# One attention and expert kernel: weight decoding in 512-column units in the first seven periods, and expert blocks that begin with 128 and 256 tokens

## The chip, the cores and the metric

The kernel runs on one core of one Trainium2 chip. The metric is the device time of one execution in microseconds (us); less is better. The core's engines are named as the profile names them: PE (TensorE, matmuls) and PEld (its weight loads), DVE (VectorE), ACT (ScalarE), POOL (GpSimd) and SP (SyncE, which here issues all transfers).

## The reference

The kernel computes an attention in which each query keeps its 32 largest scores, and feeds the result to a product of four weight matrices. With 8 batches, 8 heads, 576 positions and heads of 64:

```
scores = scale * np.matmul(q, k.transpose(0, 1, 3, 2))
kth = np.partition(scores, -top_k, axis=-1)[..., -top_k:-top_k + 1]
scores = np.where(scores >= kth, scores, -1000000000.0)
attn = softmax(scores)                      # over the keys
x = np.matmul(attn, v), laid out as 4608 tokens x 512
out = ((x @ w1) * (x @ w2)) @ w3 @ w_out    # w1, w2: 512x1024, w3: 1024x1024, w_out: 1024x512
```

The four weights arrive as 64-bit floats, so that the kernel must turn each into a 32-bit one.

## The kernel before

**Periods.** The attention is cut into 144 slots, 18 for each batch: one slot is the work of one pair of heads on 128 queries (of two pairs on the last 64). One loop, `for p in range(-1, n_slots + 3)`, runs one period for each p and is software-pipelined: period p computes the scores of slot p+1 (`scores`, tile `st` on PE, copied to `s` by ACT), finds the 32 largest of slot p (`top32_steps`, tiles `w` and `top` on DVE), masks and exponentiates slot p-1 (`mask` and `exps`, tile `pab`, on ACT and POOL) and turns and multiplies slot p-2 by the values (`turn`, `values`, tiles `tp`, `pts`, `pr`, `ro`), whose result `normalise` scales on DVE. Every engine takes its instructions in program order (class `InOrder`): an instruction that waits holds up all that stand behind it on its engine. In the trace a period begins with the first `w<-s` row of DVE.

**Expert products.** When a block of tokens is complete, `moe_steps` yields its 288 matmuls one by one: 24 groups of 8 times 24 over w1 and w2 (tile `ab`; weights `wh` and `wl`, the high and low parts) and 4 times 24 for the output (tile `eo`, weights `wf`). Before the change all blocks have 12 slots, which is 384 tokens (`NB`, the columns of each matmul). `fill(n)` puts n of these matmuls into the program at three places of a period (`SHARE = 8, 8, 8`), so a block takes 12 periods. Evictions (`take_a`, `take_b`, `take_o`) are put off to the next `fill`. Block 0 is complete at the end of period 13 and begins in period 14; the last block's matmuls run after the last period.

**Decoding.** `startup` lists the weights as units of 256 columns: 16 of w_out, 32 of w3, 16 of w1, 16 of w2. `warm()` is called six times in a period, from period 0 on. Each call starts one unit and moves every unit under way one step further: ACT writes `t` and `r` from the fetched tile `z`; DVE makes sign and magnitude (TENSOR_SCALAR, SCALAR_TENSOR_TENSOR); POOL adds the low part; then PE multiplies a w3 unit by w_out into the PSUM tile `pf` (`load_w3`), or ACT and POOL split a w1 or w2 unit into `wh` and `wl` (`load_w12`). When all of one `pf` is there, ACT copies it to `wf[0]` and DVE subtracts into `wf[1]`. Each of these stages has a `yield` of its own, and there is one more `yield` between POOL's add and the use. The tile `z` comes out of the pool `g`, which the expert products use later, `t` and `pf` out of the PSUM pool `ps_m` of three banks, which they use too.

Of the kernel before, what the change touches and what calls it, by code (L numbers as in the profile page):

```python
# [26 lines left out]
NB = 384  # L27
# [10 lines left out]
BLOCK = NS * NB // S  # L38
# [4 lines left out]
WAITING = 4  # L43
SHARE = 8, 8, 8
# [23 lines left out]
def attn_moe(ctx: ExitStack, tc: tile.TileContext, q, k, v, w1, w2, w3, w_out, out, flag, general):  # L68
# [8 lines left out]
    g_p = ctx.enter_context(tc.tile_pool(name="g", bufs=NFC))  # L77
# [3 lines left out]
    ps_m = ctx.enter_context(tc.tile_pool(name="ps_m", bufs=3, space=PSUM))  # L81
# [18 lines left out]
    def fetch(src):  # L100
        z = g_p.tile([128, 2 * NB], F32, tag="g", name="z")
        sp.dma_start(z[:, :512].bitcast(I32), src)
        return z

    bank = []

    def decode(z, dst=None):
        if not bank:
            both = ps_m.tile([128, 512], F32, tag="mm", name="t")
            bank.extend((both[:, 256:], both[:, :256]))  # L110
        t = bank.pop()
        high = z[:, 1:512:2]
        low = z[:, :512].bitcast(U16)[:, 1:1024:4]
        sign, u, r = (z[:, i * 256 : (i + 1) * 256].bitcast(I32) for i in range(3))
        act.activation(t, high, AF.Copy, scale=2.0**-112)
        act.activation(r, low, AF.Copy, scale=2.0**-13)
        yield
        ti = t.bitcast(I32)
        dve.tensor_scalar(sign, ti, -(2**31), None, op0=ALU.bitwise_and)
        dve.scalar_tensor_tensor(u, ti, 3, sign, op0=ALU.logical_shift_left, op1=ALU.bitwise_or)  # L120
        yield
        dst = z[:, :256] if dst is None else dst
        pool.tensor_tensor(dst.bitcast(I32), u, r, op=ALU.add)
        yield
        yield
        return dst

    def load_w12(i, c, z):
        if len(wl) == i:
            wl.append(const.tile([128, NCC * DF], F32R, tag="wl1", name="wl1"))  # L130
        cut = slice(c * 256, (c + 1) * 256)
        y = yield from decode(z)
        act.copy(wh[i][:, cut], y)
        yield
        pool.tensor_tensor(wl[i][:, cut], y, wh[i][:, cut].bitcast(F32), op=ALU.subtract)
# [6 lines left out]
    def load_w3(c, z):  # L142
        f, i = c // 4, c % 4
        y = yield from decode(z)
        if i == 0:
            fold[f] = ps_m.tile([128, 512], F32, tag="mm", name=f"pf{f}")
        for j in range(2 * i, 2 * i + 2):
            pe.matmul(
                fold[f], y[:, (j % 2) * 128 : (j % 2 + 1) * 128], wo[:, j * DM : (j + 1) * DM],
                start=(j == 0), stop=(j == NFC - 1),  # L150
            )
        if i == 3:
            cut = slice(f * DM, (f + 1) * DM)
            yield
            act.copy(wf[0][:, cut], fold[f])
            yield
            dve.tensor_tensor(wf[1][:, cut], fold[f], wf[0][:, cut].bitcast(F32), op=ALU.subtract)

    startup = [(w_out[c], lambda z, c=c: load_wout(c, z)) for c in range(16)]
    for f in range(NFC):  # L160
        startup += [(w3[c], lambda z, c=c: load_w3(c, z)) for c in range(4 * f, 4 * f + 4)]
        startup += [(w1[c], lambda z, c=c: load_w12(0, c, z)) for c in range(2 * f, 2 * f + 2)]
    startup += [(w2[c], lambda z, c=c: load_w12(1, c, z)) for c in range(16)]
# [171 lines left out]
    def moe_steps(xs, nb, places, after):  # L335
# [34 lines left out]
        for e in range(NEC):  # L370
            p = ps_m.tile([128, 512], F32, tag="mm", name="eo")
# [57 lines left out]
    n_blocks = n_slots // BLOCK  # L429
    column, places = {}, []  # L430
    for n in range(n_blocks):
        mine = sorted({group_of[i] for i in range(n * BLOCK, (n + 1) * BLOCK)}, key=lambda g: groups[g])
# [9 lines left out]
        assert lo == NB  # L442
# [54 lines left out]
    for hp in range(NHP):  # L497
        kts[0, hp] = load_k(0, hp)
        if hp == 0:
            prefetch(WAITING)  # L500
    for hp in range(NHP):
        vts[0, hp] = load_v(0, hp)
    renew_q(1)
    for p in range(-1, n_slots + 3):
        i, j, m = p + 1, p - 1, p - 2
        finder = top32_steps(ss[p], p) if 0 <= p < n_slots else iter(())
# [16 lines left out]
        fill(SHARE[0])  # L523
# [8 lines left out]
        fill(SHARE[1])  # L532
# [20 lines left out]
        fill(SHARE[2])  # L553
        for _ in finder:
            pass
        if 0 <= m < n_slots:
            n = m // BLOCK
# [8 lines left out]
            if (m + 1) % BLOCK == 0:  # L566
# [3 lines left out]
    while queue:  # L570
        fill(6)
# [5 lines left out]
    wp = ps_m.tile([128, 512], F32, tag="mm", name="wp")  # L577
# [57 lines left out]
```

## Time and profile before

| | |
|---|---|
| median of 3 runs (lowest to highest) | 1322.38 us (1319.78 to 1322.73) |
| the profiled execution's own time | 1321.85 us |
| its span, first to last instruction | 1320.0 us |
| PE, DVE, ACT, POOL busy | 94%, 90%, 73%, 65% of the span |
| instructions | 28196 |

The busy share says in which part of the span an engine had an instruction under way. It is a mean over stages: the periods in which weights are decoded, those with expert products beside the attention, and the expert products alone at the end. In the trace period 0 begins at 7.38 us, period 14 at 206.35, period 26 at 304.40.

### The profile page before, as it was taken

What the parts mean: (1) busy time and instruction counts of PE and PEld (TensorE: products, weight loads), DVE (VectorE), ACT (ScalarE), POOL (GpSimd) and SP (SyncE); (2) the same over time, 40 slices, a digit from 0 to 9 for tenths busy, and PEclk for the clock granted to TensorE, in tenths of its full rate; (3) what the DMA queues carried; (4) which work ended last, traced back from release to release, by engine and by line L of the source; (5) the groups of instructions that cost most, each with busy time, mean ns of one, the idle gap of its engine ahead of it and who ended that gap; (6) DMA issues with size and microseconds to landing.
All of it is one profiled execution on the core that took longest, in us unless ns stands there. A gap on an engine that the chain in (4) does not pass through costs nothing.

```text
span 1320.0 us, 28196 instructions
## 1 busy us (share of the span) xinstructions
PE 1235.3 (94%) x9617; PEld 1047.7 (79%) x9617; DVE 1194.1 (90%) x4012; ACT 965.9 (73%) x2057; POOL 853.7 (65%) x1225
## 2 busy tenths in 40 slices
PE   2788858999999999999999999999999999999996
PEld 1334436888888888888888888888888888888996
DVE  7988898999999999999999999999999999999610
ACT  5766786877777877777877877778777778777621
POOL 4767697666766766667757757757667666667510
PEclk9899967999999999999999999999999999999998
DMA  6333331200121001100120012110220012000000
GB/s 243 91 101 123 110 96 29 81 22 21 29 74 32 9 27 64 53 27 16 39 84 20 10 33 79 32 33 10 65 60 9 15 47 81 22 21 1 13 13 27
DMA packets 35886, 64.82 MB, mean 49 GB/s; under 512 B 6036, under 2 KB 12180, under 8 KB 35732
## 3 DMA queue, kind: packets, MB, share of 16 engines
q1 hardware_dynamic: 35732, 62.93, 15.3%
q8 instruction: 77, 1.26, 0.4%
q14 instruction: 77, 0.63, 0.2%
HBM read 53.48 MB, written 9.44 MB: 48 GB/s over the span
## 4 chain that ended last, share of the span: by engine, by line
PE 87%; DVE 4%; POOL 3%; ACT 2%; issue 2%; DMA 1%; SPq 0%; POOLq 0%
PE ab L57 32%; PE eo L57 16%; PE ro L57 15%; PE st L57 12%; PE tp L57 9%; PE pf L57 3%; DVE z L57 2%; DVE w L57 1%; POOL z L57 1%; DVE top L57 1%; POOL wl L57 1%; ACT pab L57 1%; DMA vt<-in_v 0%; ACT s L57 0%; ACT z L57 0%
## 5 line engine op out<-in xcount | busy, mean ns | idle before, releaser
L57 POOL TENSOR_TENSOR pab<-s,pab 128x576 f32<-128x576 f32 x288 | 404.2, 1426 | 127.5 <-DVE w L57 102.0
L57 DVE MAX8 top<-w 128x8 f32<-128x192 f32 (+1 forms) x1152 | 467.3, 447 | 0.0
L57 PE MATMUL ab<-x,wh 128*128 128x384 f32 x1536 | 403.7, 344 | 0.0
L57 ACT COPY pts<-tp 128x1024 f32<-128x1024 f32 x144 | 146.1, 1014 | 198.2 <-PE tp L57 196.8
L57 DVE MATCH_REPLACE8 w<-top,w 128x192 f32<-128x192 f32 x864 | 289.4, 343 | 0.0
L57 PEld LDWEIGHTS ab<-x,wh 128*128 128x128 f32 x1536 | 275.3, 189 | 0.0
L57 PE MATMUL ab<-x,wl 128*128 128x384 f32 x768 | 269.5, 351 | 0.0
L57 ACT ACTIVATE pab<-pab,edge 128x576 f32<-128x576 f32 x288 | 226.8, 787 | 0.5 <-POOL pab L57 0.5
L57 PE MATMUL eo<-g,wf 128*128 128x384 f32 x1152 | 225.8, 346 | 0.0
L57 ACT ACTIVATE pab<-s,edge 128x576 f32<-128x576 f32 x288 | 207.6, 768 | 7.6 <-POOL edge L57 7.5
L57 PE MATMUL st<-kt,qt 64*128 64x288 f32 (+1 forms) x1280 | 188.7, 443 | 18.4 <-ACT pts L57 7.4
L57 PEld LDWEIGHTS eo<-g,wf 128*128 128x128 f32 x1152 | 198.6, 188 | 7.5 <-issue 7.5
L57 ACT COPY s<-st 128x576 f32<-128x576 f32 x288 | 184.4, 640 | 19.5 <-PE st L57 19.5
L57 DVE TENSOR_TENSOR w<-w,s 128x384 f32<-128x384 f32 x288 | 183.9, 639 | 4.9
L57 DVE TENSOR_TENSOR w<-s 128x384 f32<-128x384 f32 x288 | 173.0, 642 | 7.4 <-ACT s L57 7.4
L57 PEld LDWEIGHTS ro<-pts,vt 128*64 128x64 f32 x2560 | 130.2, 139 | 51.3 <-ACT g L57 28.3
L57 PEld LDWEIGHTS st<-kt,qt 64*128 64x128 f32 (+1 forms) x1280 | 100.6, 183 | 81.0 <-ACT pr L57 28.1
L57 PE MATMUL ro<-pts,vt 128*64 128x128 f32 (+1 forms) x2560 | 163.4, 271 | 0.0
L57 PE MATMUL tp<-ident,pab 128*128 128x128 f32 x1152 | 152.1, 275 | 11.3 <-ACT s L57 11.3
L57 PEld LDWEIGHTS ab<-x,wl 128*128 128x128 f32 x768 | 144.3, 188 | 13.4 <-issue 12.3
L57 PEld LDWEIGHTS tp<-ident,pab 128*128 128x128 f32 x1152 | 136.4, 142 | 22.3 <-POOL wo L57 10.7
L57 POOL TENSOR_TENSOR g<-asb,g 128x384 fp32r<-128x384 f32 x96 | 96.9, 1010 | 86.8 <-ACT g L57 86.8
(51 smaller groups left out, 1309.6 us busy)
## 6 DMA issues: line engine op xcount, KB each, us to landing
z<-in_w SPq DMA_DIRECT2D x64, 256.0 KB, 2.7
vt<-in_v SPq DMA_DIRECT2D x32, 352.0 KB, 3.7
qt<-in_q SPq DMA_DIRECT2D x40, 256.0 KB, 2.7
kt<-in_k SPq DMA_DIRECT2D x32, 320.0 KB, 3.1
out_t<-osb SPq DMA_DIRECT2D x32, 192.0 KB, 1.9
z<-in_wo SPq DMA_DIRECT2D x16, 256.0 KB, 3.9
out_t<-osb SPq DMA_DIRECT2D x16, 160.0 KB, 1.8
out_t<-osb SPq DMA_DIRECT2D x16, 32.0 KB, 1.6
```

What stands on the lines that cost most here:

```text
L57: ins = fn(*args, **kw)
```

## The change

Decoding units have 512 columns instead of 256 (`CHUNK`), so there are 40 instead of 80: 8 of w_out, then eight times two of w3 and one of w1, then 8 of w2. They live in pools of their own, `z` (three buffers each of `z`, `r`, `y`) and `ps_e` (two banks of `t`, one of `pf`), which `settle()` closes before the first expert product; `g` and `ps_m` open then. `warm()` also runs in period -1. Several stages of a unit now share one call of `warm()`: DVE's two instructions and POOL's add stand in one step, `wh` and `wl` in another, and the spare `yield` is gone. Keys and values of the first batch are fetched one by one in the first periods instead of all ahead of the loop.

The expert blocks end at the slots in `CUTS`: 0, 4, 12, 24, and so on, so block 0 has 128 tokens, block 1 has 256, the others 384 as before. Each has 288 matmuls still, and `begin` divides them over the fills that lie between its start and the next block's: 12 for each fill for block 0 (periods 6 to 13), 8 for all others.

```
-BLOCK = NS * NB // S
+CUTS = [0, 4] + list(range(NS * NB // S, B * NS + 1, NS * NB // S))
-WAITING = 4
-SHARE = 8, 8, 8
+CHUNK = 512
+WAITING = 3
...
+    early = ExitStack()
+    z_p = early.enter_context(tc.tile_pool(name="z", bufs=WAITING))
+    ps_e = early.enter_context(tc.tile_pool(name="ps_e", bufs=2, space=PSUM))
...
     def decode(z, dst=None):
+        t = ps_e.tile([128, CHUNK], F32, tag="t", name="t")
+        r = z_p.tile([128, CHUNK], I32, tag="r", name="r")
+        act.activation(t, z[:, 1 : 2 * CHUNK : 2], AF.Copy, scale=2.0**-112)
+        act.activation(r, z.bitcast(U16)[:, 1 : 4 * CHUNK : 4], AF.Copy, scale=2.0**-13)
         yield
+        y = z_p.tile([128, CHUNK], F32, tag="y", name="y")
+        ti, yi = t.bitcast(I32), y.bitcast(I32)
+        dve.tensor_scalar(yi, ti, -(2**31), None, op0=ALU.bitwise_and)
+        dve.scalar_tensor_tensor(yi, ti, 3, yi, op0=ALU.logical_shift_left, op1=ALU.bitwise_or)
-        yield
-        dst = z[:, :256] if dst is None else dst
-        pool.tensor_tensor(dst.bitcast(I32), u, r, op=ALU.add)
-        yield
+        dst = y[:] if dst is None else dst
+        pool.tensor_tensor(dst.bitcast(I32), yi, r, op=ALU.add)
         yield
         return dst
...
     def load_w3(c, z):
-        f, i = c // 4, c % 4
+        f, i = c // 2, c % 2
         y = yield from decode(z)
         if i == 0:
-            fold[f] = ps_m.tile([128, 512], F32, tag="mm", name=f"pf{f}")
+            fold[f] = ps_e.tile([128, 512], F32, tag="pf", name=f"pf{f}", bufs=1)
-        if i == 3:
+        if i == 1:
             cut = slice(f * DM, (f + 1) * DM)
             yield
             act.copy(wf[0][:, cut], fold[f])
-            yield
             dve.tensor_tensor(wf[1][:, cut], fold[f], wf[0][:, cut].bitcast(F32), op=ALU.subtract)
...
     def begin():
         while starting:
+            if not late:
+                while going:
+                    warm()
+                settle()
             n = starting.pop(0)
-            queue.append(moe_steps([xs[n, hp] for hp in range(NHP)], NB, places[n], put_off.append))
+            fills = 3 * (CUTS[n + 2] - CUTS[n + 1]) if n + 1 < n_blocks else 36
+            steps = moe_steps([xs[n, hp] for hp in range(NHP)], widths[n], places[n], put_off.append)
+            queue.append((steps, -(-3 * (2 * NCC * NFC + NFC * NEC) // fills)))
...
     def warm():
-        if p < 0:
-            return
```

Where it stands on PE in a period that folds w3 (`pf`, numbered by fold). Before, the rows of one such period:

```order
L57 MATMUL tp_583<-ident_85,pab_434 128x128 x8
L57 MATMUL ro_592<-ident_85,pab_434 128x128
L57 MATMUL ro_592<-ident_85,wide_561 128x128
L57 MATMUL pf1_601<-wo_102,z_426 128x512 x2
L57 MATMUL pf1_601<-wo_102,z_445 128x512 x2
L57 MATMUL st_625<-kt_116,qt_130 128x288 x2
L57 MATMUL st_628<-kt_116,qt_130 128x288 x2
L57 MATMUL ro_592<-pts_595,vt_126 64x128 x8
L57 MATMUL ro_592<-pr_597,vt_126 64x128 x2
L57 MATMUL pf1_601<-wo_102,z_477 128x512 x2
L57 MATMUL pf1_601<-wo_102,z_490 128x512 x2
```

And in the changed kernel, from one fold's first unit to the end of the next fold:

```order
L57 MATMUL pf5_610<-wo_102,y_588 128x512 x4
L57 MATMUL tp_629<-ident_85,pab_441 128x128 x8
L57 MATMUL ro_638<-ident_85,pab_441 128x128
L57 MATMUL ro_638<-ident_85,wide_602 128x128
L57 MATMUL pf5_610<-wo_102,y_615 128x512 x4
L57 MATMUL st_678<-kt_106,qt_185 128x288 x2
L57 MATMUL st_681<-kt_106,qt_185 128x288 x2
L57 MATMUL ro_638<-pts_641,vt_286 64x128 x8
L57 MATMUL ro_638<-pr_643,vt_286 64x128 x2
L57 MATMUL pf6_702<-wo_102,y_668 128x512 x4
L57 MATMUL pf6_702<-wo_102,y_707 128x512 x4
```

A period held eight `pf` matmuls of one fold; it now holds sixteen of two, one fold around `tp` and ahead of `st`, the next behind `ro`.

The same stretch on DVE. Before, the first half of a period:

```order
L57 RECIPROCAL sums<-sums 128x2
L57 TENSOR_TENSOR w<-s 128x2x192 x2
L57 TENSOR_TENSOR w<-w,s 128x2x192 x2
L57 TENSOR_SCALAR z<-t 128x256
L57 SCALAR_TENSOR_TENSOR z<-t,z 128x256
L57 TENSOR_TENSOR wf_101<-pf_601,wf_100 128x512
L57 TENSOR_SCALAR z<-t 128x256
L57 SCALAR_TENSOR_TENSOR z<-t,z 128x256
L57 MAX top_97<-w 128x8 x2
```

In the changed kernel, the second half of a period (`pf_610` is fold 5), up to the next period's RECIPROCAL:

```order
L57 TENSOR_TENSOR wf_101<-pf_610,wf_100 128x512
L57 TENSOR_SCALAR y<-t 128x512
L57 SCALAR_TENSOR_TENSOR y<-t,y 128x512
L57 MAX top_95<-w 128x8 x2
L57 MATCH_REPLACE w<-top_95,w 128x192 x2
L57 TENSOR_SCALAR y<-t 128x512
L57 SCALAR_TENSOR_TENSOR y<-t,y 128x512
L57 MAX top_95<-w 128x8 x2
L57 TENSOR_TENSOR pr<-ro,pr 128x128
L57 TENSOR_SCALAR y<-t 128x512
L57 SCALAR_TENSOR_TENSOR y<-t,y 128x512
L57 RECIPROCAL sums<-sums 128x2
```

The subtraction into `wf`, which needs a whole fold from PE, stood once in a period, right after the first unit; it now stands twice, at the period's beginning and in its middle.

## Rows read from the trace of the kernel before
**Rows 1.** The page of the profiled execution: its span, the busy time of the engines, and from the 40 equal slices the busy tenths of PE and the granted TensorE clock in tenths (PEclk).

```profile
span 1320.0 us, 28196 instructions
...
PE 1235.3 (94%) x9617; PEld 1047.7 (79%) x9617; DVE 1194.1 (90%) x4012; ACT 965.9 (73%) x2057; POOL 853.7 (65%) x1225
...
PE   2788858999999999999999999999999999999996
...
PEclk9899967999999999999999999999999999999998
```

**Rows 2.** Busy time by stage. Columns: the stretch, its length, busy us and instructions of PE, PEld, DVE, ACT and POOL, granted clock, share of the DMA engines, GB/s. The stretches: period 0; periods 4 to 10; periods 11 to 13; period 14; periods 15 to 25; period 26; period 29.

```profile
7.38:18.19 10.81, 4.58 (x16) 2.45 (x16) 10.60 (x35) 4.49 (x12) 2.91 (x4) 1.00 1.04 390
56.78:165.14 108.36, 85.65 (x380) 42.20 (x379) 92.91 (x275) 75.62 (x182) 74.80 (x105) 0.94 0.36 107
165.14:206.35 41.21, 24.02 (x128) 15.22 (x126) 37.38 (x112) 33.01 (x82) 38.47 (x55) 0.63 0.28 77
206.35:216.45 10.10, 7.13 (x40) 5.49 (x41) 7.87 (x27) 5.51 (x10) 6.27 (x10) 0.66 0.08 19
216.45:304.40 87.95, 87.95 (x824) 77.49 (x824) 85.23 (x297) 69.21 (x148) 59.29 (x85) 1.00 0.16 50
304.40:312.33 7.93, 7.93 (x64) 6.99 (x64) 7.55 (x29) 5.91 (x12) 4.40 (x8) 1.00 0.11 33
328.20:336.13 7.93, 7.93 (x64) 7.00 (x63) 7.90 (x30) 6.30 (x13) 6.12 (x10) 1.00 0.01 3
```

**Rows 3.** Groups of instructions in periods 4 to 10 (56.78 to 165.14 us): busy time, mean ns of one, idle time before them and what ended it.

```profile
L57 PE MATMUL pf<-wo,z 128*128 128x512 f32 x114 | 59.8, 660 | 20.5 <-POOL z L57 18.6 <-DVE z L57 1.9
...
L57 POOL TENSOR_TENSOR z<-z 128x256 int32<-128x256 int32 x42 | 31.7, 769 | 17.1 <-ACT x L57 9.7 <-ACT t L57 2.2 <-DVE sums L57 1.7
...
L57 DVE SCALAR_TENSOR_TENSOR z<-t,z 128x256 int32<-128x256 int32 x43 | 18.3, 424 | 1.5
...
L57 DVE TENSOR_SCALAR z<-t 128x256 int32<-128x256 int32 x42 | 17.5, 417 | 5.7 <-ACT z L57 5.7
...
L57 DVE TENSOR_TENSOR wf<-pf,wf 128x512 fp32r<-128x512 f32 x7 | 4.8, 681 | 0.0
...
L57 ACT CAST wf<-pf 128x512 fp32r<-128x512 f32 x7 | 4.1, 587 | 7.2 <-PE pf L57 7.2
```

**Rows 4.** Waits in the same periods: who waited for whom, us in total, how often, the longest.

```profile
PE pf L57 <- POOL z L57: 18.6, 7, 2.9
...
DVE pr L57 <- POOL sums L57: 8.1, 7, 1.9
```

**Rows 5.** The engines in order of time in period 9 (134.40 to 150.59 us). Columns: start, time from the first to the last of a run of equal instructions, engine, operation, out<-in, how many, and in brackets the idle time before and what ended it. A matmul on 32-bit operands stands as two records.

```profile
133.91 2.31 PE L57 MATMUL pf<-wo,z 128*128 128x512 f32 x5
...
135.49 0.51 POOL L57 TENSOR_TENSOR edge<-top,coef 128x4 f32<-128x4 f32 x1
...
136.25 0.59 ACT L57 CAST wf<-pf 128x512 fp32r<-128x512 f32 x1 [1.04 <-PE pf L57]
...
136.83 0.62 POOL L57 COPY wide<-sums 128x128 f32<-128x128 f32 x1
...
138.54 2.77 POOL L57 TENSOR_TENSOR pab<-s,pab 128x576 f32<-128x576 f32 x2 [1.10 <-ACT pab L57]
...
139.39 0.61 DVE L57 MAX8 top<-w 128x8 f32<-128x192 f32 x2
...
140.57 0.41 DVE L57 TENSOR_SCALAR z<-t 128x256 int32<-128x256 int32 x1
...
142.74 3.23 PE L57 MATMUL pf<-wo,z 128*128 128x512 f32 x4 [2.61 <-POOL z L57]
...
145.64 1.41 DVE L57 MAX8 top<-w 128x8 f32<-128x576 f32 x2
...
145.89 1.64 PE L57 MATMUL st<-kt,qt 64*128 64x288 f32 x8
...
150.59 0.54 DVE L57 TENSOR_TENSOR w<-s 128x384 f32<-128x384 f32 x1
```

**Rows 6.** PE and its weight loads in order of time late in the span, with the columns of rows 5: expert products of 384 columns, then the transposes of a slot, then expert products again.

```profile
1202.69 0.52 PE L57 MATMUL ab<-x,wh 128*128 128x384 f32 x2
...
1205.17 0.34 PE L57 MATMUL ab<-x,wl 128*128 128x384 f32 x1
1205.34 1.03 PE L57 MATMUL tp<-ident,pab 128*128 128x128 f32 x8
...
1206.33 0.30 PEld L57 LDWEIGHTS ab<-x,wh 128*128 128x128 f32 x2
```

**Rows 7.** The first microseconds in order of time, with the columns of rows 5 (SPq is the queue of transfers), and the rate of the transfers in 40 slices of the first 30 us.

```profile
1.68 1.84 SPq L57 DMA_DIRECT2D z<-in_wo  x4
...
4.38 2.29 PE L57 MATMUL st<-kt,qt 64*128 64x288 f32 x8 [4.38 <-DMA kt<-in_k]
...
7.24 0.41 ACT L57 ACTIVATE t<-z 128x256 f32<-128x256 f32 x1
...
GB/s 0 0 98 330 383 369 350 399 367 382 386 385 402 398 402 406 399 394 402 393 385 385 385 352 243 172 0 131 219 0 0 0 11 22 167 314 401 194 232 68
```

**Rows 8.** Groups of the whole span, with the columns of rows 3.

```profile
L57 POOL TENSOR_TENSOR pab<-s,pab 128x576 f32<-128x576 f32 x288 | 404.2, 1426 | 127.5 <-DVE w L57 102.0
...
L57 POOL TENSOR_TENSOR g<-asb,g 128x384 fp32r<-128x384 f32 x96 | 96.9, 1010 | 86.8 <-ACT g L57 86.8
```

More of the change, by code (lines that the diff above doesn't have):

```diff
@@ L80, in attn_moe, with settle @@
     ps_v = ctx.enter_context(tc.tile_pool(name="ps_v", bufs=1, space=PSUM))
-    ps_m = ctx.enter_context(tc.tile_pool(name="ps_m", bufs=3, space=PSUM))
+    early = ExitStack()
+    z_p = early.enter_context(tc.tile_pool(name="z", bufs=WAITING))
+    ps_e = early.enter_context(tc.tile_pool(name="ps_e", bufs=2, space=PSUM))
+    late = {}
+    def settle():
+        early.close()
+        late["g"] = ctx.enter_context(tc.tile_pool(name="g", bufs=NFC))
+        late["mm"] = ctx.enter_context(tc.tile_pool(name="ps_m", bufs=3, space=PSUM))
     ident = const.tile([128, 128], F32, name="ident")
@@ L370, in moe_steps @@
         for e in range(NEC):
-            p = ps_m.tile([128, 512], F32, tag="mm", name="eo")
+            p = late["mm"].tile([128, 512], F32, tag="mm", name="eo")
             for f in range(NFC):
@@ L428, in attn_moe @@
         group_of.append(len(groups) - 1)
-    n_blocks = n_slots // BLOCK
-    column, places = {}, []
+    n_blocks = len(CUTS) - 1
+    block_of = [n for n in range(n_blocks) for _ in range(CUTS[n], CUTS[n + 1])]
+    column, places, widths = {}, [], []
     for n in range(n_blocks):
-        mine = sorted({group_of[i] for i in range(n * BLOCK, (n + 1) * BLOCK)}, key=lambda g: groups[g])
+        mine = sorted({group_of[i] for i in range(CUTS[n], CUTS[n + 1])}, key=lambda g: groups[g])
         lo, pieces = 0, []
@@ L451, in evict, with fill @@
             put_off.pop(0)()
-    def fill(n):
+    def fill():
         evict()
+        n = queue[0][1] if queue else 0
         while queue and n:
-            if next(queue[0], "end") == "end":
+            if next(queue[0][0], "end") == "end":
                 queue.pop(0)
@@ L496, in attn_moe @@
     renew_q(0)
[L497 to L503, printed above, removed]
+    kts[0, 0] = load_k(0, 0)
+    prefetch(WAITING)
     for p in range(-1, n_slots + 3):
         i, j, m = p + 1, p - 1, p - 2
+        if i + 1 < NHP:
+            kts[0, i + 1] = load_k(0, i + 1)
+        if 0 <= p < NHP:
+            vts[0, p] = load_v(0, p)
+        if p == 0:
+            renew_q(1)
         finder = top32_steps(ss[p], p) if 0 <= p < n_slots else iter(())
@@ L570, in attn_moe @@
     while queue:
-        fill(6)
+        queue[0] = queue[0][0], 6
+        fill()
     evict()
@@ L576, in attn_moe @@
     dve.tensor_reduce(worst[:, :1], worst[:, 1:], axis=AX.X, op=ALU.max)
[L577 removed]
+    wp = late["mm"].tile([128, 512], F32, tag="mm", name="wp")
     pe.transpose(wp[: B + 1, :128], worst, ident)
```

58 lines of the change are left out of this document (22 added, 36 removed).

## The prediction, made before the changed kernel ran

> **What bounds the kernel now.** I read the page first, then busy time by stage, then the groups and waits of the decoding stage, then one of its periods in order of time. On the page PE is busy nine tenths or more in nearly every slice, except in the first seven and in the tail, and the granted clock dips only there [rows 1]. So there are two stages with different limits. From period 15 on PE is never idle: period 26 takes 7.93 us with PE busy for all of it and DVE for 7.55; in periods with `take_b`, such as 29, DVE has 7.90 [rows 2]. PE bounds them, and DVE is right behind. In the decoding stage nobody is full: periods 4 to 10 take 108.4 us, 15.5 each, with DVE busy 92.9 and PE 85.7 [rows 2]. There the engines wait for each other: PE's `pf` matmuls for POOL's add, 18.6 us, and DVE's `normalise` for `sums`, 8.1 [rows 4]. Period 9 shows the chain: ACT and POOL reach `pab` late, POOL's add stands behind it, `pf` starts at 142.74 after 2.61 us of idle PE, `st` stands behind `pf`, and the period ends with what hangs on `st` [rows 5].
>
> What the change can move lies ahead of 304.40: from period 26 on the order is the old one. Before, periods 0 to 13 end at 206.35, and periods 14 to 25 take 10.10 + 87.95 = 98.05 [rows 2].
>
> **Prices of a 512-column unit.** DVE: 417 and 424 ns at 256 columns, and the subtraction into `wf`, also from PSUM, 681 at 512 [rows 3]; so 0.68 each, 1.35 for the two (before 0.84 for half as many columns). POOL: 769 ns at 256 [rows 3], 1010 at 384 and 1426 at 576 [rows 8], so about 1.27 for an add or a split. [...] Four matmuls are eight records, 3.44. ACT's copy to `wf` is 0.59, DVE's subtraction 0.68 [rows 3].
>
> **Part 1, less decoding work.** 80 units at 0.84 were 67 us of DVE, 40 at 1.35 are 54: 13 us less. That is a gain only if DVE stays fed.
>
> **Part 2, twice the columns in each period.** A period with folds has on DVE 7.55 of attention, six units and two `wf`: 7.55 + 8.1 + 1.36 = 17.0. On PE it has four w3 units, 13.8, and some 3.7 of attention (below): 17.5. If it ran at these sums it would beat two old periods of 15.5. But the stages now stand in one step, and there is one `pf` bank, so I follow one loop. Take as X the moment at which DVE ends the `wf` in the middle of a period.
> - Behind it DVE has three units (4.05), a MAX and MATCH_REPLACE set (139.39 to 140.57, 1.18), the MAX8 over 576 (1.4) and `pr` and `sums` (0.3) [rows 5]: the next period begins at X + 6.9.
> - The next fold needs from X one unit of DVE and POOL, 2.7, and two units of PE back to back, 6.9: it ends at X + 9.6, which is 2.7 into the new period. ACT 0.6 and DVE 0.68 later its `wf` is done, at 4.0. DVE has nothing else to do in between than the four `w`, 2.5.
> - The first unit of the fold after that: DVE to 5.3, POOL to 6.6. Then POOL has `edge` to `wide` (135.49 to 137.45, 1.96) and the two `pab` (2.77) [rows 5] before it comes to the second unit's add, done at 12.6. PE has done the first unit and `tp` by 11.1.
> - PE's second unit ends at 16.0, ACT and DVE follow: the next X, at 17.35.
>
> So a period with folds takes 6.9 + 17.35 = 24.3 us, 7 more than any engine's sum: DVE waits some 5 us for the `wf` in the middle. The unknown is how tight the loop is. Below, the old stage's ratio of period to DVE's busy time, 108.36 / 92.91 = 1.166 [rows 2], gives 19.8; above, PE at its lower clock (rival 4). I take the loop, since the rows of order show each link.
>
> The start: ACT now has four units ahead of the first copies of `s`. Keys, queries and four units are 2.7 MB, and transfers came to some 385 GB/s from 2 us on [rows 7]: the fourth lands at about 9, `s` is there at 12, and DVE reaches period 0 behind a fifth unit at about 14 instead of 7.4. Period 0 is DVE's: 6.4 of attention (10.60 less five old units at 0.84 [rows 2]) and six units, 14.5, to 28.5. Period 1 has the first fold, which PE begins cold (eight `st` records took 2.29 us at 4.38 [rows 7], and 1.64 at 145.89 [rows 5]): PE ends it some 6.6 into the period, which makes it 27, to 55.5. Periods 2 and 3 take 24.3 each, to 104. In period 4 POOL's `sums` stands behind adds and splits of w2 units, 26, to 130. Period 5 is POOL's: five adds and six splits, 14.0, `edge` to `pab` 4.7, and 2.7 of waiting for the first unit, 21.5, to 151.5. I add 2 us for dips of the clock: period 6 begins at 153.5.
>
> **Part 3, expert products of 128 and 256 columns.** Fourteen matmuls of 384 columns begin between 1202.69 and 1205.17, 0.177 each [rows 6]; 24 of them are 4.25 of 7.93, which leaves 3.7 for the attention. No row has such a matmul with fewer columns. Below, a third of 0.177 is 0.059; but each needs its weights, and two loads of `ab` in a row take 0.30 with 0.19 for one, so 0.11 apart, and eight transposes of 128 columns start 0.109 apart [rows 6]. [...] I take 0.112, since a load of the same shape went at that pace. Then a period of block 0 has 36 x 0.112 + 3.7 = 7.7 on PE and about 7.75 on DVE, and takes 7.9: eight periods are 63, and 2 for a cold beginning, as period 14 took 10.10 [rows 2]: 65, to 218.5. [...]
>
> Block 1 at 256 columns, two thirds of 0.177, has PE at 6.5 a period; DVE then sets it, 7.55 without `take_b` and about 7.8 with: 93 us for twelve periods, 5 less than the 98.05 before.
>
> **The sum.** 153.5 + 65 + 93 = 311.5 against 304.4: 7.1 us longer. The profiled execution took 1321.85 us at a span of 1320.0, half a microsecond below the median of the runs; so 1329. The eight periods of block 0 and the compressed decoding cost more than the old 14 periods, and block 1 gives 5 back.
>
> The tail is not touched: the last block has 384 tokens and nothing beside it, as before. Transfers are covered: six units and what else is due are under 4 MB a period, 10 us at 385 GB/s, under the 15 of the shortest; keys and values now stand on SP's queue behind fetches of `z` that wait for a free buffer, but the first values are due in period 2 only.
>
> **Rivals.**
> 1. *The decoding is better overlapped, and the kernel is faster.* At the old stage's ratio periods 1 to 4 take 19.8 each, 79 instead of 101.6, and period 5 POOL's 18.7: 25 us less, 1304. For it speaks that the old stage hid most such waits; against it that old `wf` stood once a period with spare steps ahead. It decides where periods 1 to 4 average under 23.6. Chance 0.24.
> 2. *A matmul does not get shorter with fewer columns* (0.177, bound by its weight load). Block 0 costs 2.3 us a period more, 18, and block 1 gives 2 less: 1350. Against it stand the loads 0.11 apart. Chance 0.10.
> 3. [...] Chance 0.08.
> 4. *PE folds at its lower clock.* By the loop PE idles some 7 us in each fold period, and in periods 11 to 13, busy 24.0 of 41.2, the granted clock was 0.63 against 0.94 in 4 to 10 [rows 2]. [...] Chance 0.08. [...]
>
> **The numbers.** My own case, 1329, has the rest, 0.50. Its own range is 1318 to 1340, from 2 us more or less in each of the five fold and last decoding periods; so a quarter of it lies within no change, and a twelfth below. A measurement of this kernel tells about 0.2%, 2.6 us. Faster: rival 1 and that twelfth, 0.28. Same: 0.12. Slower: 0.60. From rival 1's value to just under rival 4's, 1304 to 1353, leaves out a half of rivals 1 and 4 and all of 3.
>
> **What would show it.** Right: periods 2 and 3 near 24 us, with DVE idle some 5 us ahead of the second `wf`; POOL nearly full in period 5; period 6 beginning near 154; `ab` matmuls of 128 columns 0.11 apart, and periods of 7.9 under block 0. Wrong: fold periods under 23; PE's granted clock near one half through periods 1 to 4; a spacing of 0.18 or 0.21; or a stall at the change of pools in period 6, for which I have put down nothing, since the last split stands ahead of period 6's `sums` on POOL.

## The result, and the profile after

The changed kernel takes 1337.24 us (median; 1335.93 to 1339.22) against 1322.35 us for the kernel before beside it: 1.0124 times as long, with a 95% interval of 1.0105 to 1.0143. The direction was forecast; the loss is 15 us where 7 were forecast, and the time lies inside the range, 8 us above 1329.

The page of the profiled execution, which took 1339.22 us (its lines as in [rows 1]):

```profile
span 1337.4 us, 28334 instructions
...
PE 1244.3 (93%) x9905; PEld 1063.7 (80%) x9905; DVE 1175.5 (88%) x3940; ACT 957.9 (72%) x1981; POOL 846.0 (63%) x1177
...
PE   2778399989999999999999999999999999999996
```

PE is below nine tenths in the first five slices (33 us each), in the ninth, and in the last; behind the ninth the two pages look alike. So the loss lies in the decoding. Busy time by stage, with the columns of [rows 2]: period 0; the fold periods 1 to 4; period 5; periods 6 to 13 (block 0); 14 to 25 (block 1); period 26:

```profile
18.49:34.33 15.84, 3.60 (x5) 1.56 (x6) 15.60 (x37) 8.48 (x15) 7.79 (x6) 1.00 0.84 286
34.33:142.93 108.60, 78.77 (x256) 36.68 (x254) 66.34 (x161) 58.36 (x108) 58.84 (x60) 0.88 0.42 135
142.93:167.28 24.35, 7.80 (x38) 4.89 (x38) 14.96 (x37) 13.08 (x25) 17.77 (x19) 0.57 0.11 35
167.28:232.04 64.76, 62.77 (x570) 55.98 (x570) 60.95 (x217) 48.43 (x106) 42.67 (x65) 0.92 0.04 12
232.04:323.64 91.60, 85.14 (x903) 72.33 (x903) 90.18 (x322) 72.93 (x160) 64.73 (x93) 0.98 0.15 49
323.64:331.49 7.85, 6.79 (x56) 5.65 (x54) 7.82 (x30) 6.21 (x14) 5.49 (x9) 1.00 0.18 50
```

Read the lengths against the prediction's. Block 0 takes 64.76 us (65 forecast), block 1 91.60 (93). Period 6 begins at 167.28 and not at 153.5: that is 13.8 us, more than the whole error, since the later stages give some of it back. It is spread: period 0 begins at 18.49 (4.5 late) and is 1.3 too long, the fold periods are 7.0 too long together, period 5 is 2.9 too long, less the 2 us put down for the clock. In the fold periods no engine is full: of 108.60 us PE is busy 78.77, DVE 66.34, and DVE's share is lower than before the change (0.61, against 0.86 by [rows 2]).

The waits in periods 2 to 4 (62.23 to 142.93 us; who waited for whom, us in total, how often, the longest):

```profile
POOL wl L57 <- ACT wh L57: 28.2, 8, 6.0
DVE wf L57 <- ACT wf L57: 21.0, 4, 6.8
...
PE pf L57 <- POOL y L57: 15.8, 5, 4.1
...
DVE sums L57 <- POOL sums L57: 8.1, 4, 2.8
```

DVE's 21.0 is the subtraction into `wf` behind a fold, which the prediction had (some 5 us a period; it is 7). The 8.1 for `sums` it had in period 4 only. Period 2, from 62.23 on, shows in order of time where they stand (columns of [rows 5]):

```profile
66.19 0.69 DVE L57 TENSOR_TENSOR wf<-pf,wf 128x512 fp32r<-128x512 f32 x1 [1.89 <-ACT wf L57]
...
68.34 1.26 POOL L57 TENSOR_TENSOR y<-y,r 128x512 int32<-128x512 int32 x1 [0.32 <-DVE y L57]
...
69.66 6.44 PE L57 MATMUL pf<-wo,y 128*128 128x512 f32 x8 [4.13 <-POOL y L57]
...
73.38 2.49 POOL L57 TENSOR_TENSOR y<-y,r 128x512 int32<-128x512 int32 x2
...
77.03 3.60 PE L57 MATMUL pf<-wo,y 128*128 128x512 f32 x8
...
81.28 0.69 DVE L57 TENSOR_TENSOR wf<-pf,wf 128x512 fp32r<-128x512 f32 x1 [6.83 <-ACT wf L57]
...
88.80 1.27 POOL L57 TENSOR_TENSOR y<-y,r 128x512 int32<-128x512 int32 x1 [1.57 <-DVE y L57]
...
90.15 0.21 POOL L57 TENSOR_SCALAR sums<-sums 128x2 f32<-128x2 f32 x1
90.40 0.17 DVE L57 RECIPROCAL sums<-sums 128x2 f32<-128x2 f32 x1 [1.76 <-POOL sums L57]
```

The first half is the loop as forecast, link by link: the first `wf` begins 3.96 us into the period and ends at 4.65 (4.0 forecast), and DVE is idle 6.83 us ahead of the `wf` in the middle. That one ends 19.75 us into the period instead of at 17.35. Two rows with the granted clock show most of the difference: the fold's first unit ran at 0.57 in the mean (0.50 from 71.00 to 74.00 us), the second at 1.00.

```profile
69.66:76.10 6.44, 6.44 (x10) 2.81 (x11) 3.59 (x14) 2.56 (x4) 5.70 (x7) 0.57 0.43 140
77.03:80.63 3.60, 3.60 (x12) 1.41 (x10) 0.00 (x0) 3.14 (x6) 0.00 (x0) 1.00 0.00 0
```

Eight `pf` records took 6.44 us and then 3.60: 2.8 us on the path, after 4.13 us in which PE had nothing. In periods 3 and 4 the first unit took 5.21 and 6.29 us, at a granted clock of 0.71 and 0.58, after the same 4.13. The second half is the part that was read wrongly. DVE's work behind `wf` ends at 88.63, 6.7 us after 81.97, as forecast; but POOL has the last unit's add from 88.80 to 90.07 and `sums` only behind it, and DVE waits 1.76 us for that.

### The profile page after: what moved, and what is told of

Its sections match the earlier page's. It is cut to its first block, busy times and chain, and to the rows that moved or that the text cites. A ratio compares the mean times of both kernels' runs of the same rounds, so it can differ in the third digit from the quotient of the medians.

```text
span 1337.4 us, 28334 instructions
## 1 busy us (share of the span) xinstructions
PE 1244.3 (93%) x9905; PEld 1063.7 (80%) x9905; DVE 1175.5 (88%) x3940; ACT 957.9 (72%) x1981; POOL 846.0 (63%) x1177
## 4 chain that ended last, share of the span: by engine, by line
PE 81%; DVE 10%; ACT 3%; POOL 3%; issue 1%; DMA 1%; SPq 0%; POOLq 0%; DVEq 0%; ACTq 0%
PE ab L57 30%; PE eo L57 15%; PE ro L57 14%; PE st L57 11%; PE tp L57 8%; DVE w L57 5%; PE pf L57 4%; DVE top L57 3%; DVE y L57 2%; POOL y L57 1%; DMA z<-in_wo 1%; ACT pab L57 1%; ACT s L57 1%; POOL wl L57 1%; POOL pab L57 0%
## 5 line engine op out<-in xcount | busy, mean ns | idle before, releaser
L57 PE MATMUL ab<-x,wh 128*128 128x384 f32 (+2 forms) x1664 | 419.2, 335 | 0.0
L57 PEld LDWEIGHTS ab<-x,wh 128*128 128x128 f32 x1664 | 292.9, 190 | 2.0 <-issue 1.5
L57 PE MATMUL ab<-x,wl 128*128 128x384 f32 (+2 forms) x832 | 283.1, 340 | 0.0
L57 PE MATMUL eo<-g,wf 128*128 128x384 f32 (+2 forms) x1248 | 232.2, 336 | 0.0
L57 ACT ACTIVATE pab<-s,edge 128x576 f32<-128x576 f32 x288 | 207.6, 768 | 20.2 <-POOL edge L57 20.2
L57 PEld LDWEIGHTS eo<-g,wf 128*128 128x128 f32 x1248 | 205.5, 189 | 8.1 <-issue 8.1
L57 PE MATMUL st<-kt,qt 64*128 64x288 f32 (+1 forms) x1280 | 184.6, 436 | 17.0 <-ACT s L57 9.4
L57 PEld LDWEIGHTS ro<-pts,vt 128*64 128x64 f32 x2560 | 129.2, 138 | 50.6 <-ACT g L57 26.6
L57 PEld LDWEIGHTS ab<-x,wl 128*128 128x128 f32 x832 | 157.3, 189 | 12.5 <-issue 11.6
L57 DVE TENSOR_TENSOR w<-s 128x384 f32<-128x384 f32 x288 | 165.5, 615 | 0.1
L57 POOL TENSOR_TENSOR g<-asb,g 128x384 fp32r<-128x384 f32 (+2 forms) x104 | 98.3, 945 | 82.7 <-ACT g L57 82.5
L57 PEld LDWEIGHTS tp<-ident,pab 128*128 128x128 f32 x1152 | 134.0, 141 | 10.8 <-ACT s L57 5.1
```

The source lines that it names most:

```text
L57: ins = fn(*args, **kw)
```

## Experiments

Each is an edit of the changed kernel. T6 is the beginning of period 6 in its profile (167.28 in the changed kernel, whose time is 1337.24). Ratios are to the kernel before, with 95% intervals. T6 comes from one execution of each kernel and contains the beginning of period 0, which lies between 16.01 and 18.49 us in five kernels with the same opening (the changed one, e3, e6, e9, e11). So the length of periods 0 to 5 is given too where steps are compared. It is 148.79 us in the changed kernel and 148.88 in e3, which decodes in the same way, though single periods of the two differ by up to 2.7.

The times of e1, e5, e6, e8, e10, e11, e14 and e15 lie outside both of the ranges expected for them, and that of e12 0.4 us above its first.

**e1: three stages given a step of their own again.** The `yield` goes back between DVE's two instructions and POOL's add, between `wh` and `wl`, and between the copy to `wf[0]` and the subtraction.

```
         dve.scalar_tensor_tensor(yi, ti, 3, yi, ...)
+        yield
         pool.tensor_tensor(dst.bitcast(I32), yi, r, op=ALU.add)
...
     act.copy(wh[i][:, cut], y)
+    yield
     pool.tensor_tensor(wl[i][:, cut], y, wh[i][:, cut].bitcast(F32), op=ALU.subtract)
...
             act.copy(wf[0][:, cut], fold[f])
+            yield
             dve.tensor_tensor(wf[1][:, cut], fold[f], ...)
```

> The changed kernel with its decoding stages in steps of their own again (a step between DVE's two instructions and POOL's add, between wh and wl, between the two copies of a fold), still six units of 512 columns in a period. Theory A (the time was lost because stages that stand in one step make the engines wait for each other inside it): the fold periods, now 25 to 28 us, come to about 20 (1.17 times DVE's 17), period 5 from 24 to 18, period 6 begins near 135 instead of 167, and the kernel takes 1300 to 1310. Rival B (the density loses it: twice the columns in a period through one pf bank and a cold PE): the fold periods stay at 24 or more and the kernel within 10 us of 1337.

1320.08 us, 0.9989 [0.9977, 1.0001]; periods 1 to 5 take 26.8, 21.7, 23.5, 23.4 and 20.2, T6 149.07. Periods 0 to 5 take 131.29 us. The stages in one step cost 17 us of the changed kernel: all that it had lost. The time lies between the two expectations; the fold periods average 23.8 us, nearer to the second (24 or more) than to the first (about 20).

**e6, e7, e9, e11: which of the three steps.** e6 has only the `yield` between `wh` and `wl`, e7 only the one ahead of POOL's add, e9 only the one ahead of the subtraction, e11 those of e6 and e9.

> The changed kernel with one step more, between ACT's wh and POOL's wl. In the changed kernel POOL waited 28 us for wh in periods 2 to 4, and 0.73 for each unit in period 5. Theory A: period 5 comes from 24.4 to about 20.5 and periods 1 to 4 lose about 2 us each, since POOL's adds no longer stand behind a wl that waits for ACT: 1324 to 1330. Rival B (POOL's wait in the fold periods is cover, since DVE and PE wait for the fold anyway): period 5 alone gets shorter, 1332 to 1335.

> The changed kernel with one step more, between DVE's two instructions and POOL's add. Theory A (each merged step costs by itself): the last unit's add no longer waits for DVE ahead of sums, periods 1 to 5 lose 1.5 to 2 us each, 1327 to 1332. Rival B (the extra step makes each fold one step longer through the one pf bank): 1336 or more.

> The changed kernel with one step more, between ACT's copy of a fold into wf and DVE's subtraction. All three added steps together brought 17 us, the other two alone 0.5 less and 5 more. Theory A (what is left is DVE's in-order wait for the fold's copy, 21 us in periods 2 to 4): this step alone shortens periods 1 to 4 by 3 to 4 us each, 1320 to 1327. Rival B (the three steps work only together, since a step won at one place is lost at the next engine): within 4 us of 1337.

> The changed kernel with two of the three steps: between wh and wl, and between the two copies of a fold; DVE's instructions and POOL's add stand in one step. Theory A (the add's own step is not needed, it cost 5 us by itself): 1315 to 1322. Rival B (the steps work only together): 1328 to 1337.

| | time, us | ratio | T6 | periods 0 to 5 | periods 1 to 5, each |
|---|---|---|---|---|---|
| e6 | 1336.85 | 1.0108 [1.0091, 1.0125] | 163.38 | 147.20 | 29.6 28.0 27.1 25.4 21.2 |
| e7 | 1342.78 | 1.0141 [1.0123, 1.0160] | 169.67 | 152.83 | 28.3 27.8 27.5 30.0 23.5 |
| e9 | 1333.08 | 1.0105 [1.0083, 1.0126] | 158.71 | 142.70 | 25.9 23.5 25.8 27.2 24.4 |
| e11 | 1326.21 | 1.0044 [1.0027, 1.0061] | 153.43 | 135.91 | 26.6 24.0 24.0 24.3 21.2 |

The subtraction alone shortens periods 0 to 5 by 6.1 us: DVE no longer stands still behind ACT's copy. The split gives period 5 its forecast length, 21.2 (21.5 forecast), but 1.6 us in all. The add alone gives nothing (they grow by 4.0), and with the other two it gives 4.6. The intervals of e6, e7 and e9 overlap with that of the changed kernel, 1.0105 to 1.0143, so no step alone is shown to change the time; the two of e11 are, and all three of e1. One wait of e6 (61.6 to 142 us), then one of e9 (61 to 140), stand where others went:

```profile
POOL y L57 <- DVE y L57: 20.7, 7, 6.3
```

```profile
DVE y L57 <- ACT t L57: 15.7, 9, 5.2
```

In e6 POOL no longer waits for `wh` but for DVE's `y`; in e9 DVE no longer waits for `wf` but for ACT's `t`. So no step is the cause by itself; where one is freed, another wait takes over. Three rows of period 5 of the changed kernel show what the split's step costs there:

```profile
155.05 0.62 ACT L57 CAST wh<-y 128x512 fp32r<-128x512 f32 x1 [1.11 <-POOL y L57]
...
155.75 1.27 POOL L57 TENSOR_TENSOR wl<-y,wh 128x512 fp32r<-128x512 f32 x1 [0.73 <-ACT wh L57]
...
156.97 1.27 POOL L57 TENSOR_TENSOR y<-y,r 128x512 int32<-128x512 int32 x1
```

POOL is done with an add, ACT copies to `wh`, and POOL stands still for that (0.73 us here, and 3.1 us over four units of period 5) because `wl` is its next instruction.

**e5: `sums` ahead of the last unit.** The last call of `warm()` in a period moves to the next period's beginning, behind `invert`.

```
         folded = next(finder, None)
         warm()
+        warm()
...
                 starting.append(n)
-        warm()
```

> The changed kernel with the last call of warm() in a period moved behind sums, reciprocal and the w instructions of the next, so that POOL's sums no longer stands behind the last unit's add. In the changed kernel DVE waited 8.1 us for sums in periods 2 to 4 and 4.8 ahead of period 6. Theory A (these waits are part of the missing 14 us): 6 to 12 us less, 1325 to 1331. Rival B (the add then stands ahead of edge and pab instead, and the loop through the mask gets longer by as much): 1333 to 1340.

1355.66 us, 1.0251 [1.0233, 1.0268]; periods 2 to 4 take 30.6, 33.6 and 31.6. The units now stand ahead of `edge` and the mask. Waits in 62 to 160 us:

```profile
DVE wf L57 <- ACT wf L57: 36.5, 6, 11.3
...
POOL sums L57 <- ACT pab L57: 9.7, 3, 3.8
```

`sums` still waits, now for ACT's `pab` through the mask, and the wait for `wf` has grown. So the 1.76 us at a period's end are in the trace, but moving the unit away costs more at the place where it then stands.

**e8: nothing decoded in period -1.**

```
     def warm():
+        if p < 0 and not ss:
+            return
```

> The changed kernel without the first four calls of warm() in period -1, so that the first scores do not stand behind four units on ACT; two units are started in that period and the last two in period 6. Theory A (the late start is time lost, and the units find room later): period 0 begins at about 8 instead of 18.5, later periods carry four units more at 2 us each, 1334 or less. Rival B (what starts early is paid for later, at the 3.5 to 4 us that a unit costs in a w2 period): 1340 to 1346.

1352.15 us, 1.0224 [1.0207, 1.0241]. Period 0 begins at 10.29 instead of 18.49, but the units missing there are still to be done when block 0 is due: period 6 takes 21.0 us, and period 7 begins at 188.54 (177.13 in the changed kernel). The units cost more in period 6 than the late beginning did.

**e2, e10: a second bank for `pf`, taken from `t`.** e2 in the changed kernel, e10 in e1.

```
-        t = ps_e.tile([128, CHUNK], F32, tag="t", name="t")
+        t = ps_e.tile([128, CHUNK], F32, tag="t", name="t", bufs=1)
-            fold[f] = ps_e.tile([128, 512], F32, tag="pf", name=f"pf{f}", bufs=1)
+            fold[f] = ps_e.tile([128, 512], F32, tag="pf", name=f"pf{f}", bufs=2)
```

> The changed kernel with two banks for pf and one for t. Theory A: the fold chain still goes through DVE's wf in the middle of the period, so periods 2 to 4 change by under 2 us each, and the single bank of t costs about as much: 1332 to 1342. Rival B (the one pf bank is what holds the next fold back): periods 2 to 4 get 4 us shorter each, 1320 to 1327.

> All three steps added, and two banks for pf with one for t. With the steps alone PE waited 10.4 us for DVE's subtraction into wf in periods 2 to 4, before the next fold could begin. Theory A (now the single bank is what holds): periods 2 to 4 come from 22.8 to about 20, 1309 to 1315. Rival B (DVE and ACT then wait for the one bank of t as long): 1317 to 1324.

e2: 1340.70 us, 1.0150 [1.0128, 1.0172]. e10: 1340.72 us, 1.0157 [1.0134, 1.0180], with periods of 27.2, 20 us slower than e1. One row of e10's waits (60.7 to 142 us) shows the price of the bank taken from `t`:

```profile
ACT t L57 <- DVE y L57: 34.3, 12, 4.1
```

So these two say nothing on the `pf` bank itself; e16 and e17 below do.

**e3: the old first blocks.** `CUTS` without the 4, so blocks of 384 tokens from slot 0 on.

> The changed kernel's decoding with the old blocks, all of 384 tokens, the first from period 14 on. By the rows of the changed kernel periods 6 to 13 then have attention alone, about 7.5 us each instead of 8.1, 5 us less, and periods 14 to 25 take 98 as in the kernel before instead of 91.6, 6.5 more: 1336 to 1341, so the split into 128 and 256 tokens is worth next to nothing either way. A theory by which the short matmuls cost the time expects under 1330.

1336.47 us, 1.0109 [1.0088, 1.0131]: the division of the first block is worth nothing either way. Periods 6 to 14 then take 7.36 us each and 15 to 25 7.8 to 8.1, and period 26 begins at 319.88.

**e4: half the columns in a period, as before.** e1's edits, e3's blocks, and a new unit only in every second call, three in a period.

```
+        calls.append(p)
-        if fetched:
+        if fetched and len(calls) % 2:
```

> Units of 512 columns, stages in steps of their own, a unit started only at every second call (three a period, as many columns as before the change), and blocks of 384 tokens alone. Theory A: DVE has 12.1 instead of 13.3 us in a decoding period, the waits are those of before, so these periods take about 14 instead of 15.5, and the kernel 1298 to 1308. Rival C (the long units themselves, their fetch and the blocks that they make in each queue, are what costs): decoding periods of 15.5 or more, 1320 or over.

1343.48 us, 1.0167 [1.0146, 1.0188]. Fold periods take 17.6 to 19.2 us, against 15.5 for the same columns in 256-column units [rows 2]. Rows of one of them:

```profile
111.81 5.17 PE L57 MATMUL pf<-wo,y 128*128 128x512 f32 x8 [5.48 <-POOL y L57]
...
117.90 1.01 ACT L57 COPY pts<-tp 128x1024 f32<-128x1024 f32 x1 [4.19 <-PE tp L57]
```

A unit of eight `pf` records stands ahead of `tp` on PE, and ACT's `pts` waits 4.19 us for it. So at the old density a fold period is 2 to 3.5 us longer than before. That it is the unit's length alone is not shown: e4 also differs from the kernel before in its buffers, its single `pf` bank and its steps, and e14 below, which takes the units out of that place, is no faster.

**e12: e1 with four `y` buffers.** The pool `o` opens with the expert products, which makes room.

```
-        y = z_p.tile([128, CHUNK], F32, tag="y", name="y")
+        y = z_p.tile([128, CHUNK], F32, tag="y", name="y", bufs=4)
```

> All three steps added, and four buffers of y instead of three (the pool o is opened late to make room). With the steps alone DVE waited in periods 2 to 4 for a free y, 7.1 us behind PE's folds and 6.5 behind POOL's wl. Theory A (the ring of y is part of the loop): periods 2 to 5 lose 2 to 3 us each, 1309 to 1315. Rival B (PE's one pf bank and its order around st decide): 1317 to 1323.

1315.37 us, 0.9955 [0.9940, 0.9970]: faster than both kernels. Period 1 falls from 26.8 us in e1 to 21.5, T6 is 143.53. That is nearly the whole gain: periods 2 to 5, which were to lose 2 to 3 us each, change by under 0.2. Its fold periods:

```profile
33.62:123.38 89.76, 71.27 (x256) 34.38 (x254) 70.09 (x161) 56.70 (x107) 59.07 (x58) 0.96 0.48 157
```

22.4 us each, against 27.2 in the changed kernel and 23.8 in e1, with the same work.

**e13, e14, e15: `tp` and `st` ahead of the fold units.** The second and fourth calls of `warm()` in a period stand behind `turn` and behind `values` (a step of DVE's search, `next(finder)`, moves along with the first of them): e13 in e12, e14 in e4 with four `y` buffers, e15 in the changed kernel.

```
-        warm()
         fill()
         begin()
-        next(finder, None)
         if 0 <= m < n_slots:
             tp, ro = turn(pabs[m][0], wide)
             pts, pr, rec = take_turned(tp, ro, wide)
+        warm()
+        next(finder, None)
...
         next(finder, None)
-        warm()
         if i < n_slots:
...
             renew(vts, load_v, m)
+        warm()
         next(finder, None)
```

> The four edits of the spaced kernel with four y buffers, and besides the second and fourth calls of a period's unit steps moved so that tp, its copies pts, the scores st and their copies stand ahead of the units on PE and ACT. Theory A: what still holds the fold periods at 21 to 23 us, above DVE's 17, is that tp and st stand behind fold units in PE's queue (ACT waited for st 16.4 us in three fold periods, up to 6.0 at once). Then periods 1 to 5 take 17 to 20 us each, period 6 begins near 130, and the time is 1300 to 1308. Rival B: it is the length of the chain through one pf bank and the units themselves, and the wait for st is only the place where it shows. Then the wait moves on to the units behind, the fold periods stay at 21 to 24, and the time is 1312 to 1320.

> As the kernel with three units a period and the old first block of 384 tokens (17.6 to 19.2 us a fold period, 1343), with four y buffers and the same two calls moved. Theory A: those periods were long because tp and st stood behind 512-column fold units in PE's queue; moved, they take 14 to 15.5, the decoding of 13 periods ends 30 to 40 us earlier, and the time is 1302 to 1313. Rival B: a 512-column unit costs its length wherever it stands, since DVE and POOL wait for it through buffers; then fold periods stay at 17 to 19 and the time is 1330 to 1345.

> The changed kernel with only the two calls moved, without any of the steps divided. Theory A: tp and st behind fold units cost each fold period 2 to 3 us by themselves; moved, periods 1 to 5 take 22 to 25 instead of 24 to 28, period 6 begins near 157, and the time is 1325 to 1331. Rival B: POOL's sums, the mask and the copies to wf stand where they did, and they end last; the periods stay at 24 to 28, and the time is 1333 to 1342.

e13: 1315.84 us, 0.9967 [0.9954, 0.9979], T6 143.12: as e12. e14: 1349.16 us, 1.0221 [1.0204, 1.0238], worse than e4 and outside both forecasts. e15: 1349.63 us, 1.0232 [1.0215, 1.0249], too. What happened stands in e14's waits (58 to 150 us) and in two rows of e15:

```profile
PE ro L57 <- POOL wide L57: 31.6, 5, 6.3
```

```profile
72.61 0.33 PE L57 MATMUL ro<-ident,wide 128*128 128x128 f32 x1 [3.67 <-POOL wide L57]
...
72.77 3.60 PE L57 MATMUL pf<-wo,y 128*128 128x512 f32 x8
```

Behind `tp` on PE stands `ro`, which needs POOL's `wide`, and POOL's `wide` stands behind adds and splits. PE now waits for that, with the fold units queued behind it. So putting `tp` and `st` first in PE's order does not shorten the periods. That a late POOL is behind either order fits these rows, but no run makes POOL earlier by itself.

**e16, e17: the `pf` bank by itself.** In e1, `t` goes into SBUF, with three `y` and two `r` buffers. e16 keeps one `pf` bank, e17 has two.

```
-        t = ps_e.tile([128, CHUNK], F32, tag="t", name="t")
+        t = z_p.tile([128, CHUNK], F32, tag="t", name="t", bufs=2)
```

> The spaced kernel, with t in two SBUF buffers instead of two PSUM banks, three y and two r buffers, and still one pf bank; it is the control for the next run. If t's place costs nothing and the buffers suffice, fold periods take 21 to 24 us as in the spaced kernel with three y buffers and the time is 1315 to 1322. If two r buffers or a reading of t from SBUF beside POOL cost, DVE's y takes more than 690 ns or ACT waits for POOL, and the time is above 1322.

> The same with two pf banks. Theory A: the loop that the prediction followed, from one fold's wf over the freed pf bank to the next fold's first unit, is what is left: PE waited 10.1 us for wf in 58 to 128 us with one bank. Then that wait goes, the fold periods fall by 2 to 3 us each, and the time is 8 to 12 us under the control's. Rival B: the units before tp and st stand in PE's queue all the same, DVE's y and POOL's add come no sooner, and the wait moves to y: within 3 us of the control.

e16: 1340.85 us, 1.0143 [1.0119, 1.0166], T6 165.65. e17: 1328.77 us, 1.0054 [1.0036, 1.0072], T6 154.57. The second bank gives 12 us, as the first of the two expectations had it. Waits in 58 to 128 us, first of e16, then of e17:

```profile
PE pf L57 <- DVE wf L57: 19.0, 5, 5.9
```

```profile
PE pf L57 <- POOL y L57: 13.8, 5, 4.4
```

PE's wait for the freed bank is gone, and what it waits for now is the next unit's `y`. e16, with `t` in SBUF, is 20 us slower than e1; more on that below.

## Why the prediction was off

**Right.** The place: the loss lies in the decoding, and the expert products cost what was put down. The 128-column matmuls begin 0.112 us apart (twelve steps from 178.16 to 179.50), as taken (0.112), and those of 256 columns 0.117, both at a granted clock of 1.00. Rows of block 0, then of block 1:

```profile
178.49 0.39 PE L57 MATMUL ab<-x,wh 128*128 128x128 f32 x2
178.72 0.28 PE L57 MATMUL ab<-x,wl 128*128 128x128 f32 x1
178.83 0.38 PE L57 MATMUL ab<-x,wh 128*128 128x128 f32 x2
```

```profile
253.11 0.40 PE L57 MATMUL ab<-x,wh 128*128 128x256 f32 x2
253.34 0.28 PE L57 MATMUL ab<-x,wl 128*128 128x256 f32 x1
253.46 0.40 PE L57 MATMUL ab<-x,wh 128*128 128x256 f32 x2
```

Three matmuls lie between the first and the last row of each. With 0.177 for 384 [rows 6], rival 2 is out; no run shows a spacing of 0.18 or 0.21 for short matmuls. The prices of a unit held: DVE 683 and 692 ns, POOL's add 1.27 us. For PE no run shows eight `pf` records in 3.44 us, or two units in the loop's 6.9: they start 0.43 apart (five in 2.31 us [rows 5], of which one alone takes 0.59), and with the last one's end eight took 3.60 in the changed kernel at a granted clock of 1.00 (77.03 to 80.63), sixteen 7.13 (from 109.91 on), and eight 6.44 at 0.57. The loop through one `pf` bank is a real bound: e17 against e16 is 12 us, and in the changed kernel DVE waits 21.0 us for `wf`, four times in three periods.

**The step that failed: "the next period begins at X + 6.9".** In periods 1 to 4 it begins 8.31, 8.51, 8.50 and 9.59 us behind the end of the `wf` in the middle, together 7.3 us more. The step counted DVE's instructions and forgot that the last unit's add on POOL stands ahead of `sums`. The prediction saw this order for period 4 and put 1.7 us there; it holds in every fold period, so 5.6 of the 7.0 us missing in the fold periods are here. The rest is in the first half of the loop, which was forecast at 17.35 and came out at 19.75, 16.64 and 17.72 in periods 2 to 4. There the lower clock of rival 4 shows, but in the fold's first unit only (6.44, 5.21 and 6.29 us at 0.57, 0.71 and 0.58, against 3.60 at 1.00); in periods 3 and 4 the first `wf` waits for nothing, which makes up for much of it. The fold periods average 0.88 of the clock, not one half. No run shows a time for rival 4, from which the range has its upper end, 1353; in periods 2 to 4 the first units took 7.1 us more together than at 3.60 each.

**The other terms that were too small.** Period 5 was made from POOL's own work, 21.5; that no other instruction stands between POOL's add and its `wl`, so that it waits 3.1 us for ACT's `wh` in four of its units, was missed, and e6 takes 3.1 us off this period (though not off the whole time). The beginning of period 0 was put at 14 from a rate of 385 GB/s, and came at 18.49 here, at 16.01 to 17.67 in the other four kernels with the same opening; rows of the start:

```profile
1.68 1.37 SPq L57 DMA_DIRECT2D z<-in_wo  x3
...
8.47 0.62 ACT L57 ACTIVATE t<-z 128x512 f32<-128x512 f32 x1 [6.46 <-DMA z<-in_wo]
...
14.25 0.63 ACT L57 ACTIVATE t<-z 128x512 f32<-128x512 f32 x1 [1.96 <-DMA z<-in_wo]
...
18.49 2.08 DVE L57 TENSOR_TENSOR w<-s 128x384 f32<-128x384 f32 x2
18.71 1.44 POOL L57 TENSOR_TENSOR wo<-y,r 128x512 int32<-128x512 int32 x1 [0.90 <-DVE y L57]
```

The first of three 512 KB fetches is used at 8.47, the fourth not before 14.25 (9 forecast): the fourth fetch is only issued at 9.69, when the first of three `z` buffers is free. The sum assumed that transfers run on; it did not ask when each could be issued. No run gave `z` a fourth buffer, so what that alone costs is not shown. In 2 to 9 us the transfers came to 324 GB/s:

```profile
2.00:9.00 7.00, 2.29 (x8) 1.26 (x8) 0.00 (x0) 0.54 (x2) 0.00 (x0) 1.00 0.94 324
```

**The sum again.** 13.8 us late at period 6, less 0.2 and 1.4 in the two blocks, is period 26 at 323.64 instead of 311.5; from there to the end of the span it is 1.8 us shorter than before, and 1329 + 12.1 - 1.8 = 1339.3 is the profiled execution's 1339.22. The median is 2 us under it.

**Rival 1** needed fold periods under 23.6; with the steps as written they are 27.2. e12 reaches 22.4 and is faster than before by 0.45%, about 6 us, not by the 18 of the rival: its fold periods are still 2.6 us each above the rival's 19.8, 10.8 in all, and its start and period 0 together are 5.1 us over the forecast. So the sizes of the change need not make the kernel slower: giving the joined stages their three steps back takes away its loss, and a fourth `y` buffer brings some 5 us more.

**Open.** Fold periods of e12 still take 22.4 us where DVE is busy 17.5. The `pf` bank may hold some of it: it did in e16, by e17, and in e12 PE still waits 10.1 us for `wf` in 58 to 128 us. A second bank without the price of `t` in SBUF or of one `t` buffer was not tried. Why POOL's add in a step of its own is worth nothing alone is not settled.

## What to carry to other kernels

When stages are joined in one step of a hand-written pipeline, look at every instruction that then waits for its direct forerunner on another engine: what is queued behind it pays, not it. A sum of each engine's work finds neither these waits nor the first instruction of the next period that stands behind the last unit on a neighbour engine, so follow the loop over every engine's queue, to the period's very first row. Here units of twice the size needed more buffers and more steps between stages than the change gave them.

## What the runs showed of the hardware

DVE's two-operand `w<-s` comes twice in a period. The second took 1.08 to 1.63 us in the periods below in which POOL had an add or a split beside it, and 0.54 to 0.56 in those in which it had not; the first took 0.54 to 0.56 in all of them. Its durations in the first 34 us of the changed kernel (min, median, max in ns):

```profile
L57 DVE TENSOR_TENSOR w<-s x2: 547/1084/1621, 18.5 to 18.9; 128x384 f32<-128x384 f32 x2
```

The long one, 1621 ns against 547, is the second of the two at 18.49, while POOL's add runs from 18.71 on. That is 1.1 of the 1.3 us by which period 0 was too long. In periods 1 and 5 the second of the two took 1623 and 1626 ns, beside an add (from 34.55 on) and a split (from 143.25 on); in periods 2 to 4 each took 536 to 552, with no add or split beside them. The kernel before shows it too, in its first 34 us:

```profile
L57 DVE TENSOR_TENSOR w<-s x6: 536/555/1089, 7.4 to 31.0; 128x384 f32<-128x384 f32 x6
```

Its two of period 0 (0.56 and 0.55 us) had no add beside them; in periods 1 and 2 the second took 1.08 to 1.09 us beside an add of 256 columns. Longer means show in e16 too, where DVE reads `t` from SBUF instead of PSUM. Groups of 58 to 128 us, first of e12, then of e16:

```profile
L57 DVE TENSOR_SCALAR y<-t 128x512 int32<-128x512 int32 x19 | 13.0, 683 | 2.5 <-ACT t L57 1.3 <-PE pf L57 1.3
L57 DVE SCALAR_TENSOR_TENSOR y<-t,y 128x512 int32<-128x512 int32 x18 | 12.4, 691 | 0.6
```

```profile
L57 DVE SCALAR_TENSOR_TENSOR y<-t,y 128x512 int32<-128x512 int32 x16 | 17.2, 1073 | 0.5
L57 DVE TENSOR_SCALAR y<-t 128x512 int32<-128x512 int32 x16 | 15.0, 936 | 12.3 <-PE pf L57 8.5 <-POOL wl L57 3.7
```

683 and 691 ns become 936 and 1073, DVE is busy 83.2 us in the fold periods instead of 71.7 (e1, 33.00 to 128.91 us), and the kernel is 20 us slower. The first one's durations lie far apart (min, median, max in ns, 58 to 128 us of e16):

```profile
L57 DVE TENSOR_SCALAR y<-t x16: 413/943/1625, 57.9 to 124.7; 128x512 int32<-128x512 int32 x16
```

The shortest of them, 413 ns, is less than the 683 out of PSUM, the longest, 1625, more than twice that. POOL's own instructions are longer in e16 as well (means of 58 to 128 us, e16 against e12): adds 1337 ns against 1293, splits 1538 against 1273, masks 1687 against 1415. The two `r` buffers of e16 may have a part in the 20 us: ACT waited 12.3 us there for POOL's `y`. No run shows what lies behind these longer durations. The price of a unit was taken from rows with `t` in PSUM, which do not show them. Period 0's was taken from a period in which no add stood beside `w<-s`, while the next ones of the same trace had it.
